# Load order of a gated spectral and MLP token mixer: gate row, tables and an x block moved, and one wait told to the planner

## The chip, the cores and the metric

The kernel runs on one core of a Trainium2 chip. The metric is the device time of one execution in microseconds (us), the median of several runs. Engines are named as the profile does: PE is TensorE (matmuls; PEld its weight loads), DVE is VectorE, ACT is ScalarE, POOL is GpSimd, SP is SyncE, which here only issues DMAs.

## The reference

The input x is 2048 tokens by 512 features. The output is g * a + (1 - g) * b, token by token, where

```
g = sigmoid((x * gate_w).sum(-1))                     # one gate per token
a = irfft2(rfft2(x) * (w_r + 1j * w_i))               # spectral filter over tokens and features
h = layernorm(x);  u = gelu(h^T w1 + b1);  b = (u w2 + b2)^T   # token MLP, 2048 -> 1792 -> 2048
```

All inputs and outputs are bf16. The Fourier transforms are done as radix-4 steps on DVE and matmuls against cosine and sine tables on PE.

## The kernel before, in words

Tokens are split as token = 512 q + 4 a + r, with a on the 128 partitions. A block j = 4 q + r is 128 tokens by 512 features. "Row r" means the four blocks of one r.

**A planner sets the order.** Each step is added as a task with an engine, an estimated duration, reads and writes under symbolic keys, a priority, and buffers that it allocates and frees (`add`, `Plan.order`). The planner runs through time and gives each engine, when it is free, the ready task of the lowest priority number. The result is one fixed list; each engine then runs its instructions in that order. The waits between engines are not the planner's: a layer below places them from the memory ranges that the instructions read and write. So a key that the planner does not know of can still be a wait in the program.

**Loads.** Nearly all loads are tasks of SP (`ld`, `load`, `ld_w1`, `load_wb`, `ld_W`) and go through one DMA queue in the order of their priorities; a few early ones go through ACT's queue. In the first third these are: x by rows; `ta`, the forward tables, one piece per row; w1 in two sets (`wa` holds its first 7 blocks of 128 columns, row by row, and `wb` the next); `flip` and the bias; `tb`, the second forward table; `gw`, the gate row, spread over all partitions; `b2h`; and W, the spectral weights, in many small pieces.

**First third.** Per row r: DVE takes LayerNorm statistics (L487, L488), and normalised blocks h are written by DVE (L521) or ACT (L527). PE accumulates the first MLP product over blocks j (L705), in the order j = 0, 8, 4, 12, 1, 5, 9, 13 and so on. Between these the forward transform runs: DVE combines the four q of a row (L535 to L542), PE multiplies by `ta` (L554 to L557), ACT evicts PSUM (L560), DVE combines again (L566, L567). DVE also multiplies x by the gate row in place (L730, once per row; the only use of `gw`), and ACT sums that to the gate's logit (L735).

**Middle.** A radix-4 over rows on DVE (L585 to L598, then the small L637), a second product on PE with `tb` (L653), eviction on ACT (L660), combination on DVE (L669 to L677), then the spectral multiplication on DVE (L820 to L846). PE fills its time with the MLP: L705, then L1008 with w2.

**First inverse.** A radix-4 on DVE for each half lt (0 and 1 of the spectrum): L590 and L591 write what the even rows r = 0, 2 read, L600 and L601 what the odd rows 1, 3 read. Then PE makes sixteen products `i1(h, r, lt)` (L895, L897 and L898 for even r, L890 for odd r) into two `fa` and two `fb` PSUM buffers, lt 0 in `fa` and lt 1 in `fb`. ACT evicts each (L906 into `ze`, L904 into `zz`); DVE combines the even ones (`zf`, L914 to L920) and makes z (`fq`, L926, L927).

**Last third.** PE makes the last inverse product (`i3`, L967 to L970), ACT scales it by the gate into `B` (L974), DVE combines it (`es`, L989 to L993) and adds it to the MLP's result (`fin2`, L1027), which ACT has evicted (L1014). The last two blocks are finished by DVE (L1021) straight from PSUM. Stores go out on SP, and the last one on ACT's queue.

Of the kernel before, what the change touches and what calls it, by code (L numbers as in the profile page):

```python
# [13 lines left out]
BF16 = mybir.dt.bfloat16  # L14
F32 = mybir.dt.float32

P = 128
S = 2048
D = 512
# [113 lines left out]
class Plan:  # L133
# [11 lines left out]
    def add(self, eng, dur, emit, reads=(), writes=(), prio=0.0, alloc=(), free=(), nbytes=0, after=(), late=0.0):  # L145
        t = Task()
        t.late = late
        t.eng, t.dur, t.emit, t.prio = eng, dur, emit, prio
        t.alloc, t.free, t.nbytes = tuple(alloc), tuple(free), nbytes
        t.users, t.end, t.ready = [], None, 0.0  # L150
        deps = set(after)
        for k in reads:
            if k in self.last_w:
                deps.add(self.last_w[k])
            self.readers.setdefault(k, []).append(t)
        for k in writes:
            if k in self.last_w:
                deps.add(self.last_w[k])
            deps.update(self.readers.get(k, ()))
            self.last_w[k] = t  # L160
            self.readers[k] = []
        deps.discard(t)
        t.deps = deps
        self.tasks.append(t)
        return t
# [73 lines left out]
def tt(n):  # L239
    return 0.07 + n / 1920.0  # L240
# [14 lines left out]
def mm(*ns):  # L255
    return sum(max(n, 120) / 2400.0 + 0.0025 for n in ns)
# [3 lines left out]
def tiny(k):  # L260
    return 0.09 * k + 0.06
# [3 lines left out]
def kernel(  # L265
# [14 lines left out]
    V, A, T = nc.vector, nc.scalar, nc.tensor  # L280
    tabs = {k: nc.inline_tensor(v, name="dft_" + k).ap() for k, v in make_tables().items()}

    rows = "(q a r) d -> a q r d"
    x4 = A_x[0].rearrange(rows, q=4, r=4)
# [17 lines left out]
    add = pl.add  # L302
    t = {}
# [39 lines left out]
    def load(key, shape, dt, src, nbytes, prio=0.0):  # L343
        def emit():
            t[key] = sb(shape, dt, key)
            dma(t[key][:], src)
        return add("SP", 0.5, emit, writes=[key], prio=prio, nbytes=nbytes)

    def ld(keys, dst, src, nbytes, prio, eng="SP"):
        return add(eng, 0.5, lambda: dma(dst(), src, A if eng == "ACT" else None), writes=keys, prio=prio, nbytes=nbytes, after=[a0])  # L350
# [21 lines left out]
    for r in range(4):  # L372
        if r == 0:
            for n, qs in enumerate(XQ):
                ld([("x", 0, q) for q in qs], lambda qs=qs: t["x"][:, qs[0]:qs[-1] + 1:2, 0, :], x4[:, qs[0]:qs[-1] + 1:2, 0, :], 131072 * len(qs), -9 + 0.1 * n)
        else:
            for qs in ((0,), (1,), (2, 3)) if r == 1 else ((0, 1, 2, 3),):
                c = slice(qs[0], qs[-1] + 1)
                ld([("x", r, q) for q in qs], lambda r=r, c=c: t["x"][:, c, r, :], x4[:, c, r, :], 131072 * len(qs), 2 * r - (3 if r == 1 else 0) + 0.01 * qs[0])
        ld([("ta", r)], lambda r=r: t["ta"][:, r, :], tabs["ta"][:, r, :], 163840, 2 * r + (0.6 if r == 1 else 0.2) if r else -0.8)  # L380

    NF = 7
    WB = (0, NF, NF + 4, NFT)
# [23 lines left out]
    def ld_bias():  # L407
        dma(t["b1b"][0:NFT], B_b1.rearrange("(t f) -> t f", f=P))
    add("SP", 0.5, ld_bias, writes=["bias"], prio=7.1, nbytes=4096, after=[a0])
    load("tb", [P, 776], BF16, tabs["tb"], 198656, prio=9)  # L410

    def ld_wb(k, q):
        def emit():
# [10 lines left out]
            add("SP", 0.5, ld_wb(k, q), writes=[("w1", k + 1, 4 * q + r) for r in range(4)], prio=10 + 12 * k + 0.1 * q,  # L424
                nbytes=131072 * (WB[k + 2] - WB[k + 1]), after=after)
    load_wb(0)
    load("gw", [P, D], BF16, gate_w[None, :].to_broadcast([P, D]), 131072, prio=14.5)

    ld(["b2h"], lambda: t["b2h"][:], B_b2.rearrange("(q p r) -> p q r", q=4, r=4), 300000, 14.6)

    wsrc = (A_w_r, A_w_i)

# [39 lines left out]
    for r in range(4):  # L472
# [3 lines left out]
        for b, qs in enumerate(groups):  # L476
# [48 lines left out]
            for j in js:  # L525
                if j in HACT:
                    add("ACT", 0.71, lambda j=j: A.activation(t["h"][:, j // 4, j % 4, :], t["x"][:, j // 4, j % 4, :], ActF.Identity,  # L527
                                                                  bias=t["nmr"][:, j:j + 1], scale=t["rstd"][:, j:j + 1]),
                        reads=xb + [("rstd", *g)] + mvk, writes=[("h", j)], prio=-0.5 + 0.1 * r)
# [19 lines left out]
        for dq in range(4):  # L549
            def fa(r=r, dq=dq):  # L550
# [10 lines left out]
                reads=[("pa", r, dq)], writes=[("X", r, dq)], prio=0, free=["fa"])  # L561
# [69 lines left out]
    for lt in (0, 1):  # L631
# [4 lines left out]
        if lt == 0:  # L636
            add("DVE", 0.15, lambda: V.tensor_copy(t["X"][:, 0, :, :, :, 0], t["fx"][:]), reads=["fx"],  # L637
                writes=[("Z", 0, 0), ("Z", 0, 1)], prio=3.0)
# [6 lines left out]
    for lt in (0, 1):  # L645
        for e in (0, 2, 1, 3):
            for c in range(2):
                tag = ("fa", "fb")[c]
# [7 lines left out]
            for c in range(2):  # L656
                tag = ("fa", "fb")[c]
# [6 lines left out]
            if e >= 2:  # L664
                def tb2(lt=lt, e0=e - 2):
# [14 lines left out]
                    writes=[("B", lt, i) for i in es_], prio=2.5)  # L680
# [47 lines left out]
    for r in range(4):  # L728
# [3 lines left out]
            reads=["gw"], writes=xk, prio=6)  # L732
# [139 lines left out]
    i1t = {}  # L872
    for rs, h in ((0, 0), (0, 1), (1, 0), (1, 1)):
        for r in (rs, rs + 2):
            for lt in range(2):
                tag = ("fa", "fb")[lt]

                def i1(h=h, r=r, lt=lt, tag=tag):
                    if "zz" not in t:
                        t["zz"] = sb([P, 2, 2, 2, 2, 2, 2, P], BF16, "X")  # L880
                        t["ze"] = sb([P, 2, 2, 2, 2, L], BF16, "h")
                    p1 = t["i1", h, r, lt] = ps([P, 2, L], F32, tag, 2)
                    o, w = ti_at(r)
                    ti = t["ti"][:, o:o + w]
                    for v in range(2):
                        d = lambda c: t["B"][:, lt, r, 2 * c + v, h:L:2]
                        if r % 2:
                            for c in range(2):
                                f = (2 * c if lt == 0 else 5 - c) * P
                                T.matmul(p1[:, v], lhsT=d(c), rhs=ti[:, f:f + L], start=(c == 0), stop=(c == 1))  # L890
                        else:
                            n = 129 if r == 0 and lt == 0 else P
                            u = ti[:, 256 * lt:256 * lt + 256]
                            if n > P:
                                T.matmul(p1[:, v], lhsT=d(1), rhs=t["ti"][:, 2816:3072], start=True, stop=False)  # L895
                            else:
                                T.matmul(p1[:, v, n:], lhsT=d(1), rhs=u[:, n:], start=True, stop=True)  # L897
                            T.matmul(p1[:, v, 0:n], lhsT=d(0), rhs=u[:, 0:n], start=(n == P), stop=True)  # L898
                i1t[h, r, lt] = add("PE", mm(*([256] * 4 if r % 2 else [128] * 4)), i1, reads=[("T", lt, r % 2), "ti"], writes=[("i1", h, r, lt)], prio=3, alloc=[tag])

                def i1ev(h=h, r=r, lt=lt):
                    if r % 2:
                        o = t["zz"][:, 1, h, lt, :, :, r // 2, :]
                        A.copy(o, t["i1", h, r, lt][:].rearrange("p v (k a) -> p v k a", k=2))  # L904
                    else:
                        A.copy(t["ze"][:, h, r // 2, lt], t["i1", h, r, lt][:])  # L906
                add("ACT", act(512), i1ev, reads=[("i1", h, r, lt)] + pbk, writes=[("zz" if r % 2 else "ze", h, r, lt)], prio=1.7, free=[tag], after=[lined])

            if r % 2 == 0:
                def zf(h=h, r=r):  # L910
                    e = t["ze"][:, h, r // 2]
                    k0, k1 = (t["zz"][:, 0, h, :, :, k, r // 2, :] for k in range(2))
                    if r == 0:
                        V.tensor_copy(k0[:, :, :, 0], e[:, :, :, 0])  # L914
                        V.tensor_copy(k1[:, :, :, 0], e[:, :, :, P])
                        V.tensor_add(k0[:, :, :, 1:P], e[:, :, :, 1:P], e[:, :, :, P + 1:L])
                        V.tensor_sub(k1[:, :, :, P - 1:0:-1], e[:, :, :, 1:P], e[:, :, :, P + 1:L])
                    else:
                        V.tensor_add(k0, e[:, :, :, 0:P], e[:, :, :, P:L])
                        V.tensor_sub(k1[:, :, :, ::-1], e[:, :, :, 0:P], e[:, :, :, P:L])  # L920
                add("DVE", 2 * tt(512) + (tiny(2) if r == 0 else 0), zf, reads=[("ze", h, r, lt) for lt in range(2)], writes=[("zz", h, r, lt) for lt in range(2)], prio=3.55)

        def fq(rs=rs, h=h):
            z = xph(h)[:, 2048 * rs:2048 * rs + 2048].rearrange("p (q v n) -> p q v n", q=4, v=2)
            a, b = (t["zz"][:, rs, h, i].rearrange("p v k r a -> p k v (r a)") for i in range(2))
            V.tensor_add(z[:, 0:4:3], a, b)  # L926
            V.tensor_sub(z[:, 1:3], a[:, ::-1], b[:, ::-1])  # L927
        add("DVE", 2 * tt(1024), fq, reads=[("zz", h, r, lt) for r in (rs, rs + 2) for lt in range(2)] + [("T", 0, 0), ("T", 0, 1), ("T", 1, 0), ("T", 1, 1)],
            writes=[("z", rs, h)] + ([] if rs else ["pp" if h else "xs"]), prio=3.6)
# [27 lines left out]
    for p in range(NJ // 2):  # L957
# [24 lines left out]
        def es(p=p, j0=j0, late=late, tb2j=tb2j):  # L982
# [8 lines left out]
            V.tensor_sub(s[:, :, 1, :, P - 1:0:-1], e[:, :, :, 1:P], e[:, :, :, P + 1:L])  # L991
            V.tensor_add(o[:, :, 0:4:3], s[:, :, :, 0], s[:, :, :, 1])
            V.tensor_sub(o[:, :, 2:0:-1], s[:, :, :, 0], s[:, :, :, 1])  # L993
        add("DVE", tiny(1) + 4 * tt(512) + (0.3 if late else 0), es, reads=(k1 + ["omg"]) if late else [],
            writes=ko if late else k1, prio=4, alloc=["es"], free=["es"], after=gates if late else ())

        for i, j in enumerate((j0, j1)):
# [78 lines left out]
```

## Time and profile before

| | |
|---|---|
| median of 3 runs | 129.49 us (129.37 to 129.72) |
| the profiled execution | 129.0 us |
| its span, first to last instruction | 127.1 us |
| busy PE, DVE, ACT | 122.3, 114.6, 81.3 us |
| granted PE clock | 1.0 throughout |
| read from HBM, written | 20.86 MB, 2.10 MB |

The durations come from the one profiled execution, whose time lies 0.49 us below the median of the runs and 1.9 us above its own span. In the profile a line number is a line of the kernel; a tile is named without its buffer number. `out<-in` is what an instruction writes and reads. Idle time in brackets stands before the instruction and names what ended it. All DMAs have line L306, that of the helper which issues them.

### The profile page before, as it was taken

The page shows a single profiled execution, that of the slowest core. Times are in us where ns is not written, and L with a number is a line of the kernel's source. Part 1 is how long each engine was busy: PE and PEld are TensorE (multiplying, and loading weights), DVE is VectorE, ACT ScalarE, POOL GpSimd, SP SyncE. Part 2 cuts the span into 40 slices and gives each one's busy share as a digit, 9 for nine tenths or more (in the row PEclk, how much of TensorE's full clock was granted, in tenths as well). Part 3 has the DMA queues.
Part 4 walks back from the last instruction along what each step waited for, and adds up shares of the span by engine and source line. Part 5 has one row for each costly group of instructions (what it writes and reads, how often), then busy time and mean ns, then how long its engine had stood idle before and what let it go on. Part 6 is the DMA issues. An engine that isn't in the chain of part 4 may idle for free.

```text
span 127.1 us, 2153 instructions
## 1 busy us (share of the span) xinstructions
PE 122.3 (96%) x756; PEld 68.9 (54%) x756; DVE 114.6 (90%) x273; ACT 81.3 (64%) x165; POOL 0.2 (0%) x4
## 2 busy tenths in 40 slices
PE   6999999999999999999999999999989999999991
PEld 2345555555555466644445555555667767655590
DVE  2789999996999999999999999999989989999951
ACT  0973789699999999999420004722389999952200
POOL 0000000000000000000000000000000000000000
PEclk9999999999999999999999999999999999999999
DMA  2999999995548946899999900000000000006451
GB/s 69 300 355 291 382 366 368 351 325 106 122 107 256 285 96 143 200 406 415 411 409 406 398 29 0 0 5 0 3 0 0 0 5 0 0 0 248 165 211 44
DMA packets 18219, 23.12 MB, mean 182 GB/s; under 512 B 2190, under 2 KB 15904, under 8 KB 18208
## 3 DMA queue, kind: packets, MB, share of 16 engines
q1 hardware_dynamic: 17616, 22.36, 52.8%
q10 hardware_dynamic: 592, 0.62, 1.6%
q8 instruction: 6, 0.10, 0.3%
q14 instruction: 5, 0.04, 0.1%
HBM read 20.86 MB, written 2.10 MB: 181 GB/s over the span
## 4 chain that ended last, share of the span: by engine, by line
DVE 37%; PE 29%; DMA 21%; SPq 8%; issue 2%; DVEq 0%
PE acc L1008 16%; DMA wa<-in_B_w_dram 12%; SPq L306 8%; DMA gw<-in_gate_w_dram 6%; DVE x L730 4%; DVE xp L828 4%; DVE st L828 3%; DMA x<-in_A_x_dram 3%; DVE st L586 3%; PE acc L705 3%; DVE xp L833 2%; DVE xp L585 2%; DVE B L840 2%; DVE xp L834 2%; PE fb L890 1%
## 5 line engine op out<-in xcount | busy, mean ns | idle before, releaser
L705 PE MATMUL acc<-h,wb 128*128 128x512 bf16 x112 | 26.9, 379 | 0.0
L1008 PE MATMUL acc<-gl,wb 128*128 128x512 bf16 (+1 forms) x98 | 24.6, 371 | 0.0
L1008 PE MATMUL acc<-gl,wa 128*128 128x512 bf16 (+1 forms) x98 | 23.8, 371 | 0.0
L1014 ACT ACTIVATE x<-acc,ombb,omg 128x512 bf16<-128x512 f32 x12 | 9.0, 777 | 21.4 <-PE acc L1008 21.4
L1008 PEld LDWEIGHTS <-wa 128*128 128x128 bf16 x126 | 13.5, 113 | 9.9
L1008 PEld LDWEIGHTS <-wb 128*128 128x128 bf16 x126 | 13.3, 113 | 9.3
L705 PE MATMUL acc<-h,wa 128*128 128x512 bf16 x64 | 17.6, 379 | 0.0
L705 PEld LDWEIGHTS <-wb 128*128 128x128 bf16 x112 | 10.7, 98 | 10.5
L705 PEld LDWEIGHTS <-wa 128*128 128x128 bf16 x112 | 10.3, 98 | 10.4 <-issue 0.8
L487 DVE BATCH_NORM_STATS2 stats<-x 128x6 f32<-128x512 bf16 x14 | 9.5, 678 | 1.9 <-DMA x<-in_A_x_dram 1.9
L560 ACT CAST xp<-fa 128x512 bf16<-128x512 f32 x16 | 9.2, 580 | 2.0 <-PE fa L557 2.0
L735 ACT ACTIVATE x<-x 128x512 bf16<-128x512 bf16 x16 | 10.2, 692 | 0.0
L721 ACT ACTIVATE gl<-acc,b1f 128x512 bf16<-128x512 f32 x11 | 7.9, 719 | 3.5 <-PE acc L705 3.5
L705 PE MATMUL fb<-h,wa 128*128 128x512 bf16 x32 | 9.7, 379 | 0.0
L527 ACT ACTIVATE h<-x,nmr,rstd 128x512 bf16<-128x512 bf16 x11 | 8.4, 807 | 1.1 <-DVE nmr L518 1.1
L705 PE MATMUL fa<-h,wa 128*128 128x512 bf16 x16 | 5.9, 381 | 0.1
L653 PEld LDWEIGHTS <-X 128*128 128x128 bf16 x64 | 4.6, 98 | 2.5 <-DVE X L637 0.7
L974 ACT ACTIVATE B<-fa,g 128x512 bf16<-128x512 f32 x8 | 5.6, 704 | 0.2 <-PE fa L970 0.2
L730 DVE TENSOR_TENSOR x<-x,gw 128x2048 bf16<-128x2048 bf16 x4 | 4.8, 1220 | 1.1 <-DMA gw<-in_gate_w_dram 1.1
L974 ACT ACTIVATE B<-fb,g 128x512 bf16<-128x512 f32 x8 | 5.7, 712 | 0.0
L356 PE MATMUL fa<-xp 128*128 128x512 bf16 x10 | 4.4, 632 | 1.2 <-DVE xp L317 1.2
L660 ACT CAST X<-fb 128x512 bf16<-128x512 f32 x8 | 5.1, 636 | 0.0
(169 smaller groups left out, 232.8 us busy)
## 6 DMA issues: line engine op xcount, KB each, us to landing
wb<-in_B_w_dram SPq DMA_DIRECT2D x11, 512.0 KB
wa<-in_B_w_dram SPq DMA_DIRECT2D x7, 512.0 KB
wa<-in_B_w_dram SPq DMA_DIRECT2D x2, 896.0 KB
wb<-in_B_w_dram SPq DMA_DIRECT2D x4, 384.0 KB
out_dram<-x SPq DMA_DIRECT2D x3, 512.0 KB
x<-in_A_x_dram SPq DMA_DIRECT2D x2, 512.0 KB
wa<-in_B_w_dram SPq DMA_DIRECT2D x2, 448.0 KB
rot<-dft_ti SPq DMA_DIRECT2D x1, 768.0 KB
```

The source lines that it names most:

```text
L306: (eng or nc.sync).dma_start(out=out_ap, in_=in_ap)
L487: V.bn_stats(out=t["stats"][:, j, :], in_=t["x"][:, j // 4, j % 4, :])
L527: add("ACT", 0.71, lambda j=j: A.activation(t["h"][:, j // 4, j % 4, :], t["x"][:, j // 4, j % 4, :], ActF.Identity, bias=t["nmr"][:, j:j ...
L560: add("ACT", act(512), lambda r=r, dq=dq: A.copy(xe(r)[:, :, :, dq, :], t["pa", r, dq][:]), reads=[("pa", r, dq)], writes=[("X", r, dq)], ...
L705: T.matmul(t["u", ft][:], lhsT=w[:, j // 4, j % 4, c * P:(c + 1) * P], rhs=t["h"][:, j // 4, j % 4, :], start=(j == jorder[0]), stop=(j == ...
L721: gelus.append(add("ACT", act(512, 1) , lambda ft=ft: A.activation(t["gl"][:, ft, :], t["u", ft][:], ActF.Gelu_apprx_tanh, bias=t["b1f"][: ...
L730: add("DVE", tt(2048), lambda r=r: V.tensor_mul(t["x"][:, :, r, :], t["x"][:, :, r, :], t["gw"][:, None, :].to_broadcast([P, 4, D])), read ...
L735: A.activation(t["x"][:, q, r, :], t["x"][:, q, r, :], ActF.Copy, accum_out=t["glog"][:, 4 * q + r:4 * q + r + 1])
L828: V.tensor_mul(o, xs, w)
L974: A.activation(eo_v(p)[:, n], t["i3", j][:], ActF.Copy, scale=t["g"][:, j:j + 1])
L1008: T.matmul(t["y", j, m][:, cs], lhsT=w[:, o, 512 * q + r:512 * q + 512:4], rhs=t["gl"][:, ft, cs], start=(ft == 0), stop=(ft == NFT - 1))
L1014: A.activation(tbuf(j).rearrange("p h d -> p (h d)"), t["y", j, 0][:], ActF.Identity, bias=t["ombb2"][:, j:j + 1], scale=t["omg"][:, j:j + 1])
```

## The change

Four edits. The third x row is loaded ahead of the second part of w1's row 1 (and the planner's numbers for the x and `ta` loads are written out in tuples). The `ta` pieces of rows 2 and 3 move behind the loads of x row 3 and of w1's row 3. `gw` moves from behind the first `wb` set to before it, and `tb` from before that set to behind it. The inverse product of r = 2 is said to read ("T", lt, 1) too, the key of the odd rows. And the planned duration of `es` is 0.2 longer; that number is only the planner's.

```diff
-                ld([("x", r, q) for q in qs], ..., 2 * r - (3 if r == 1 else 0) + 0.01 * qs[0])
-        ld([("ta", r)], ..., 2 * r + (0.6 if r == 1 else 0.2) if r else -0.8)
+                ld([("x", r, q) for q in qs], ..., (0, -0.9 if len(qs) > 1 else -1 + 0.01 * qs[0], 2.503, 4.6)[r])
+        ld([("ta", r)], ..., (-0.8, 2.505, 6.3, 7.3)[r])
...
-    load("tb", [P, 776], BF16, tabs["tb"], 198656, prio=9)
+    load("tb", [P, 776], BF16, tabs["tb"], 198656, prio=14.7)
...
-    load("gw", [P, D], BF16, gate_w[None, :].to_broadcast([P, D]), 131072, prio=14.5)
-    ld(["b2h"], ..., 300000, 14.6)
+    load("gw", [P, D], BF16, gate_w[None, :].to_broadcast([P, D]), 131072, prio=7.2)
+    ld(["b2h"], ..., 300000, 14.9)
...
-  i1t[h, r, lt] = add("PE", ..., i1, reads=[("T", lt, r % 2), "ti"], ...)
+  i1t[h, r, lt] = add("PE", ..., i1, reads=[("T", lt, r % 2), "ti"] + ([("T", lt, 1)] if r == 2 else []), ...)
...
-        add("DVE", tiny(1) + 4 * tt(512) + (0.3 if late else 0), es, ...)
+        add("DVE", 0.2 + tiny(1) + 4 * tt(512) + (0.3 if late else 0), es, ...)
```

The queue's order of loads from the first `ta` on, before and after (w1 a, b: its row 1 for q = 0, 1 and q = 2, 3; w1 2, 3: its rows 2 and 3):

```
before: ta0  w1a  w1b  ta1  x2   ta2  w1_2  x3  ta3  w1_3  flip  bias  tb   wb x4       gw  b2h
after:  ta0  w1a  x2   ta1  w1b  w1_2  x3   ta2  w1_3  flip  bias  gw   ta3  wb x4       tb  b2h
```

On PE the instructions are the same in kind and order; the product `i1(1, 0, 1)` changes places with `i1(0, 2, 1)`. ACT's evictions follow that. On DVE the combinations `zf` of r = 2 come after those of r = 0 of both halves, and in the last third two `es` are followed by two `fin2`.

More of the change, by code (lines that the diff above doesn't have):

```diff
@@ L378 @@
                 c = slice(qs[0], qs[-1] + 1)
-                ld([("x", r, q) for q in qs], lambda r=r, c=c: t["x"][:, c, r, :], x4[:, c, r, :], 131072 * len(qs), 2 * r - (3 if r == 1 else 0) + 0.01 * qs[0])
-        ld([("ta", r)], lambda r=r: t["ta"][:, r, :], tabs["ta"][:, r, :], 163840, 2 * r + (0.6 if r == 1 else 0.2) if r else -0.8)
+                ld([("x", r, q) for q in qs], lambda r=r, c=c: t["x"][:, c, r, :], x4[:, c, r, :], 131072 * len(qs), (0, -0.9 if len(qs) > 1 else -1 + 0.01 * qs[0], 2.503, 4.6)[r])
+        ld([("ta", r)], lambda r=r: t["ta"][:, r, :], tabs["ta"][:, r, :], 163840, (-0.8, 2.505, 6.3, 7.3)[r])
     NF = 7
@@ L426 @@
     load_wb(0)
-    load("gw", [P, D], BF16, gate_w[None, :].to_broadcast([P, D]), 131072, prio=14.5)
-    ld(["b2h"], lambda: t["b2h"][:], B_b2.rearrange("(q p r) -> p q r", q=4, r=4), 300000, 14.6)
+    load("gw", [P, D], BF16, gate_w[None, :].to_broadcast([P, D]), 131072, prio=7.2)
+    ld(["b2h"], lambda: t["b2h"][:], B_b2.rearrange("(q p r) -> p q r", q=4, r=4), 300000, 14.9)
     wsrc = (A_w_r, A_w_i)
@@ L898, in i1 @@
                             T.matmul(p1[:, v, 0:n], lhsT=d(0), rhs=u[:, 0:n], start=(n == P), stop=True)
-                i1t[h, r, lt] = add("PE", mm(*([256] * 4 if r % 2 else [128] * 4)), i1, reads=[("T", lt, r % 2), "ti"], writes=[("i1", h, r, lt)], prio=3, alloc=[tag])
+                i1t[h, r, lt] = add("PE", mm(*([256] * 4 if r % 2 else [128] * 4)), i1, reads=[("T", lt, r % 2), "ti"] + ([("T", lt, 1)] if r == 2 else []), writes=[("i1", h, r, lt)], prio=3, alloc=[tag])
                 def i1ev(h=h, r=r, lt=lt):
@@ L993, in es @@
             V.tensor_sub(o[:, :, 2:0:-1], s[:, :, :, 0], s[:, :, :, 1])
-        add("DVE", tiny(1) + 4 * tt(512) + (0.3 if late else 0), es, reads=(k1 + ["omg"]) if late else [],
+        add("DVE", 0.2 + tiny(1) + 4 * tt(512) + (0.3 if late else 0), es, reads=(k1 + ["omg"]) if late else [],
             writes=ko if late else k1, prio=4, alloc=["es"], free=["es"], after=gates if late else ())
```

## The prediction

> **What bounds the kernel now.** I read the page's busy times first, then the timeline of TensorE (PE), then the list of waits, and last the timelines of VectorE (DVE) and ScalarE (ACT) around the waits found.
>
> ```profile
> PE 122.3 (96%) x756; PEld 68.9 (54%) x756; DVE 114.6 (90%) x273; ACT 81.3 (64%) x165; POOL 0.2 (0%) x4
> ```
>
> PE is at work in 96% of the span, and the change touches neither a matmul nor its shape. So the time can change only where PE stands still, and it stands still little. I took PE's starts one after the other: a 128x512 matmul starts 0.216 us after the one before it, a 128x128 one 0.055 us. What exceeds that is lost. From the first real matmul (5.56 us) to the last (124.06) the losses add up to 3.5 us, and half of that lies in six places: 0.23 at 6.9, 0.19 at 12.0, 0.14 at 16.7, 0.27 at 32.4, 0.33 at 44.8 and 0.55 at 93.1. The last three, in PE's timeline (start, length, what, idle and its releaser):
>
> ```profile
> 32.38 0.22 PE L556 MATMUL fa<-rot,gl 128*128 128x128 bf16 x1
> 32.69 0.23 PE L557 MATMUL fa<-rot,gl 128*128 128x128 bf16 x1
> ...
> 43.25 1.67 PE L705 MATMUL acc<-h,wb 128*128 128x512 bf16 x7
> 45.09 0.40 PE L653 MATMUL fa<-tb,X 128*128 128x128 bf16 x4 [0.16 <-DVE X L637]
> ...
> 93.00 0.22 PE L898 MATMUL fb<-rot,B 128*128 128x128 bf16 x1
> 93.61 0.23 PE L897 MATMUL fb<-rot,B 128*128 128x128 bf16 x1 [0.39 <-DVE B L601]
> ```
>
> Read the starts, not the bracket (the bracket counts from the modelled end). 32.69 - 32.38 - 0.055 = 0.26. Seven matmuls from 43.25 would end their turn at 44.76; L653 starts at 45.09: 0.33. 93.61 - 93.00 - 0.055 = 0.55. Sum 1.14 us. DVE releases all three. Why it is late is seen in its own timeline:
>
> ```profile
> 28.96 0.69 DVE L536 TENSOR_TENSOR gl<-x 128x1024 bf16<-128x1024 bf16 x1
> 30.74 1.23 DVE L730 TENSOR_TENSOR x<-x,gw 128x2048 bf16<-128x2048 bf16 x1 [1.09 <-DMA gw<-in_gate_w_dram]
> ...
> 32.22 0.42 DVE L542 TENSOR_TENSOR gl<-st 128x512 bf16<-128x512 bf16 x1
> ...
> 44.78 0.25 DVE L637 CAST X<-fx 128x32 bf16<-128x32 f32 x1
> ...
> 92.87 0.69 DVE L601 TENSOR_TENSOR B<-st 128x1024 bf16<-128x1024 bf16 x1
> ```
>
> DVE idles 1.09 us for the gate row (L730), and from there to L637 it has no other gap. L542 (end 32.64) releases L557, L637 (end 45.03) releases L653. So the first two stalls hang on one late 128-KB load.
>
> **The loads.** In the trace's landing records the loads of one queue end in the order of their issue, the slowest of the 16 rings at: w1 row 1 first part 12.63, second part 13.80, `ta` 1 14.25, x row 2 15.75, `ta` 2 16.19, w1 row 2 18.64, x row 3 20.11, `ta` 3 20.56, w1 row 3 23.05, flip 23.25, `tb` 23.70, first wb 25.12, last wb 30.02, gw 30.72. The steps between them are each load's price in the stream. In the new order: x row 2 at 12.63 + 1.50 = 14.1, `ta` 1 14.6, w1's second part + 1.17 = 15.75, w1 row 2 18.2, x row 3 19.7, `ta` 2 20.1, w1 row 3 22.6, flip 22.8, gw + 0.7 = 23.5, `ta` 3 23.9, the wb's 0.3 later than before, `tb` about 30.8. The bytes and the number of DMAs are the same, and every issue still waits on the load eight before it, so the W loads behind them shift by at most 0.3.
>
> Who needs them: gw at 29.6 (6 us early now); `ta` 1 at 16.41 (1.8 early, was 2.2); w1's second part at 16.88, where PE starts block j=9 (1.1 early, was 3.1); `ta` 2 at 24.8; `ta` 3 at 32.16; `tb` at 45.09, L653 (14 early); the first wb at 35.9. SP has nothing else in line there. x rows 2 and 3 come earlier to a DVE that is busy anyway (first use 16.24 and 21.87): worth nothing. So the moves cost nothing, and only w1's second part gives up real cover; if that goes, each microsecond of delay is one of PE.
>
> **The gate row.** DVE starts L730 at 29.65 instead of 30.74. Two later DVE steps wait for ACT's eviction of row 2 (ended 32.75, DVE then at 33.7) and row 3 (36.16, DVE at 36.2, and ACT too is 0.25 earlier): covered. So L542 ends at 31.55, ahead of L557's turn at 32.43: +0.26. L637 ends at 43.94, PE wants L653 at 44.76 - 0.26 = 44.50: +0.33. PE is 0.59 early from there. Does it keep that? The next bound is ACT. It gains 0.25 behind PE's first gain, then 0.27 where it idles for PE:
>
> ```profile
> 49.03 0.69 ACT L721 ACTIVATE gl<-acc,b1f 128x512 bf16<-128x512 f32 x1 [0.27 <-PE acc L705]
> ...
> 51.98 0.65 ACT L660 CAST X<-fb 128x512 bf16<-128x512 f32 x1
> ```
>
> 0.52 in all. PE's L653 at 50.35 to 52.77 wait for buffers that ACT evicts, with 0.12 to 0.18 of room, and PE runs only 0.07 further ahead than ACT: it just fits. DVE's L669 at 52.66 started 0.03 after ACT's eviction (51.98 + 0.65), so from there DVE keeps 0.52 of its 1.09. From 53 to 91 PE waits for nothing that is short: w2 blocks land 1.85 us or more ahead of first use, and L741 has 0.98 on ACT.
>
> **The first inverse.** Before, PE takes product (h0, r2, lt1) right after (h0, r0, lt1); its wait is on L601, the last step of the radix-4, though r2's rows were written earlier: L600 and L601 write strided rows whose span covers them. The new read of ("T", lt, 1) tells the planner this. In the built program PE's rows are the same in kind, but (h1, r0, lt1) has changed places with (h0, r2, lt1): the wait on L601 now stands behind two products and one L1008 and four L890 matmuls, 1.1 us later. In the new time PE comes there at 93.58, and L601 ends at 93.55 - 0.52 = 93.0. So the 0.55 goes. What is late next: ACT evicts each product (0.48 us from one to the next) into `ze` and `zz`, and PE waits for the buffer two before. From 91.24 on ACT needs sixteen evictions and one L1014 (0.68): 8.3 us, ended at 99.5; PE's buffer waits keep 0.04 to 0.2 of room by the same sum. Behind the moved wait stand PE's own next products and, through them, ACT's evictions; it is met before PE reaches it, so nobody waits. DVE now combines r0 of both halves first and then waits for the eviction of (h0, r2, lt1), at 95.6: it idles 0.5 there, and `z` of half 1 is ready at 99.6 instead of 99.85. PE's first L967 needs the first half of it at 99.67 (100.81 - 1.14) and the second at 99.84: 0.2 of room. I take no loss, with 0.2 as the upper bound.
>
> **The planner's 0.2 for `es`.** No instruction changes; DVE's tail order does: two `es`, then two L1027 sums. Same work, 18.2 us from 102.59 to 120.83; starting 0.6 earlier it ends at 120.2, ahead of need except 0.15 at the first L1021, which has 0.8 behind it. The sums come up to 1.3 us later, and with them one 512-KB store (115.5 instead of 114.51), which nothing waits for: the last 512-KB store landed at 124.04, the last of all at 126.19. Cost 0.
>
> **Sum.** 0.26 + 0.33 + 0.55 = 1.14 us. The profiled execution took 129.0 (span 127.1 and 1.9 around it): it becomes 127.9. The median of the runs is 0.49 above the profiled one; I keep that: 129.49 - 1.14 = 128.35, rounded 128.4.
>
> **Rivals.**
> (a) One of the gains is taken back by ACT. For it: ACT's room is 0.04 to 0.2 us at a dozen buffer waits. Against: in all of them ACT itself moves with PE. If the swap gives nothing (or another wait on `B` stands in its place), PE's 0.59 shrinks to DVE's 0.52: 129.0. If the buffers hold PE to ACT's old pace only in part, 0.3 to 0.6 are lost: 128.7 to 129.0. The Trainium skill's page "Perfetto Trace Analysis" (section "Optimization Strategy") says that consistent bubbles can mean that SBUF or PSUM is too small for the next tile; by it this case would be the likelier. The trace speaks against it for before: none of the three stalls was released by ACT.
> (b) Nothing moves: the stalls are taken up by some wait that the profile shows as covered, total gain under 0.39: 129.1 to 129.9. Against: PE has no second row of waits within 0.5 us.
> (c) Slower: w1's second part comes late. It decides from a landing after 16.8; from 18.4 on it eats both gains and is seen as slower. For it: the first part of the same row took 2.8 us of the stream where the second took 1.17. Price: rings spread 2.1 us between the first and the last; if the three loads did not overlap their ends, it would land at 15.75 + 2 x 2.1 = 19.95, PE would stand for 3.1 us, and the time be 131.5. Against: 448 KB landed 1.17 us behind its predecessor, with the ends overlapped. The Trainium skill's page "DMA: Bandwidth & Descriptors" (section "Anatomy of one DMA") fits one DMA of the GpSimd path as 2.0 us plus its bytes over 436 GB/s; paid three times in a row, as an estimate, that would be 8.6 us and slower still, and the trace's 1.17 contradicts such a sum for queued loads.
>
> **How the numbers follow.** Forecast 0.60, (a) 0.20, (b) 0.08, (c) 0.12. A difference of 0.3% (0.39 us) is about what a measurement of this kernel can tell from no change, so the forecast and (a) count as faster: 0.80. The forecast's own range is 128.1 to 128.6 (0.2 lost; 0.25 gained, should unprofiled runs have waited more for gw). With (a) it reaches 129.1, and a margin of 0.1 for the runs' scatter gives 128.0 to 129.2.
>
> **What would show it.** In the new profile: L730 with no wait for gw, at 29.6; L557 0.06 behind L556; no idle at L653; the wait on L601 gone from PE's list; L1014 and i3 (L967) starting 1.1 earlier. Wrong would be: idle of PE at about 16.9 with a wait for `wa`; new gaps of PE at L890 or L897 released by ACT; the first L967 waiting for DVE.

## The result and the profile after

The changed kernel takes 127.75 us (median of 5 runs, 127.68 to 128.01) against 129.37 for the kernel before on the same chip. The ratio is 0.9899, 95% interval 0.9867 to 0.9931, so the gain is 1.31 us (0.89 to 1.72). A second series on another occasion gave 127.95 against 129.11 and 0.9898 (0.9864 to 0.9932). Forecast were 1.14 us and 128.4.

The profiled execution took 128.01 us with a span of 126.2. Its busy times, its chain that ended last (shares by engine), and PE's whole list of waits:

```profile
PE 121.4 (96%) x743; PEld 68.9 (55%) x756; DVE 114.4 (91%) x273; ACT 81.0 (64%) x165; POOL 0.2 (0%) x4
```

```profile
PE 93%; DMA 3%; ACTq 1%; issue 1%; DVE 0%
```

```profile
PE fa L356 <- DVE xp L317: 1.2, 1, 1.2
```

Before, the same chain read "DVE 37%; PE 29%; DMA 21%": it ran over the gate row and the stalls. Now it is PE's own work. The shares alone prove little: e3 below has no stall either, and its chain reads "PE 56%; DMA 30%; SPq 11%". PE's one listed wait is that of its warm-up matmuls for a memset. Thirteen matmul records are missing from this trace (743 of 756), and each looks like a gap of 0.05 us in PE's timeline, or like 0.22 too much between two starts; those are not stalls.

The three places of the prediction, in PE's timeline (start, length, what):

```profile
32.14 0.22 PE L556 MATMUL fa<-rot,gl 128*128 128x128 bf16 x1
32.20 0.22 PE L557 MATMUL fa<-rot,gl 128*128 128x128 bf16 x1
...
43.94 1.03 PE L705 MATMUL acc<-h,wb 128*128 128x512 bf16 x4
44.80 0.39 PE L653 MATMUL fa<-tb,X 128*128 128x128 bf16 x4
...
93.42 0.60 PE L890 MATMUL fa<-rot,B 128*128 128x256 bf16 x4
93.86 0.22 PE L897 MATMUL fb<-rot,B 128*128 128x128 bf16 x1
```

L557 follows L556 by 0.06. Four L705 from 43.94 end their turn at 44.80, and L653 starts there. The moved product starts at 93.86, four L890 (0.11 each) behind 93.42. And DVE around them:

```profile
29.27 0.69 DVE L536 TENSOR_TENSOR gl<-x 128x1024 bf16<-128x1024 bf16 x1
29.87 1.22 DVE L730 TENSOR_TENSOR x<-x,gw 128x2048 bf16<-128x2048 bf16 x1
...
31.34 0.42 DVE L542 TENSOR_TENSOR gl<-st 128x512 bf16<-128x512 bf16 x1
...
43.91 0.26 DVE L637 CAST X<-fx 128x32 bf16<-128x32 f32 x1
...
92.57 0.69 DVE L601 TENSOR_TENSOR B<-st 128x1024 bf16<-128x1024 bf16 x1
...
95.97 0.42 DVE L919 TENSOR_TENSOR X<-h 128x512 bf16<-128x512 bf16 x1 [0.41 <-ACT h L906]
```

L730 no longer waits (the gate row landed at 22.26). L601 ends at 93.26, 0.60 ahead of the product that reads it.

**Two executions must be set at the same start.** Row 1's first L554 on PE started at 16.41 us before and at 16.72 after, for reasons that lie ahead of the change: row 0's first L554 differs as much (11.23 and 11.54), and no load that was moved had landed by then. From there to PE's last start it is 107.65 us before (124.06 - 16.41) and 106.48 after (123.20 - 16.72): 1.17 gained, where 1.14 was forecast. This stretch turned out to be the sharpest instrument of the study: in all seven profiles in which PE has no stall in it, it is 106.48 or 106.49. (0.14 us that PE stands ahead of j=9 in every profile, before and after, are part of it; a stall there is counted over them.)

| kernel | first L554 of row 1 | from it to PE's last start | over 106.48 | PE's stalls in it, added |
|---|---|---|---|---|
| before | 16.41 | 107.65 | 1.17 | 0.26 + 0.33 + 0.55 = 1.14 |
| after | 16.72 | 106.48 | 0 | none |
| e1 | 16.64 | 107.81 | 1.33 | 0.74 + 0.56 = 1.30 |
| e2 | 16.52 | 107.02 | 0.54 | 0.19 + 0.33 = 0.52 |
| e3 | 16.78 | 106.48 | 0 | none |
| e4 | 16.83 | 107.85 | 1.37 | 0.17 + 0.28 + 0.33 + 0.56 = 1.34 |
| e5 | 16.66 | 106.48 | 0 | none |
| e6 | 16.66 | 110.50 | 4.02 | 2.42, and 1.59 of slow matmuls |
| e7 | 16.86 | 106.49 | 0.01 | none |
| e8 | 16.97 | 106.49 | 0.01 | none |
| e9 | 16.81 | 106.49 | 0.01 | none |
| e10 (after again) | 16.89 | 106.48 | 0 | none |
| e11 | 16.98 | 107.34 | 0.86 | 0.84 |
| e12 | 17.15 | 107.13 | 0.65 | 0.63 |

### The profile page after: what moved, and what is told of

Same layout as the page of the kernel before. It is cut to its first block, busy times and chain, and to the rows that moved or that the text cites. A ratio compares the mean times of both kernels' runs of the same rounds, so it can differ in the third digit from the quotient of the medians.

```text
span 126.2 us, 2141 instructions
## 1 busy us (share of the span) xinstructions
PE 121.4 (96%) x743; PEld 68.9 (55%) x756; DVE 114.4 (91%) x273; ACT 81.0 (64%) x165; POOL 0.2 (0%) x4
## 4 chain that ended last, share of the span: by engine, by line
PE 93%; DMA 3%; ACTq 1%; issue 1%; DVE 0%
PE acc L1008 32%; PE acc L705 30%; PE fb L705 5%; PE fb L1008 5%; PE fa L705 3%; DMA wa<-in_B_w_dram 3%; PE fa L554 2%; PE fb L653 2%; PE fa L653 2%; PE fa L890 2%; PE fb L890 1%; PE fa L555 1%; ACTq L306 1%; PE fa L557 1%; PE fa L556 1%
## 5 line engine op out<-in xcount | busy, mean ns | idle before, releaser
L705 PE MATMUL acc<-h,wb 128*128 128x512 bf16 x108 | 25.9, 379 | 0.1
L1008 PE MATMUL acc<-gl,wb 128*128 128x512 bf16 (+1 forms) x94 | 24.0, 371 | 0.2
L1008 PE MATMUL acc<-gl,wa 128*128 128x512 bf16 (+1 forms) x97 | 23.8, 371 | 0.1
L1008 PEld LDWEIGHTS <-wa 128*128 128x128 bf16 x126 | 13.5, 113 | 9.9
L1008 PEld LDWEIGHTS <-wb 128*128 128x128 bf16 x126 | 13.3, 113 | 9.3
L705 PE MATMUL acc<-h,wa 128*128 128x512 bf16 x62 | 17.5, 382 | 0.1
L705 PEld LDWEIGHTS <-wb 128*128 128x128 bf16 x112 | 10.7, 98 | 10.5
L705 PEld LDWEIGHTS <-wa 128*128 128x128 bf16 x112 | 10.3, 98 | 10.7 <-DMA wa<-in_B_w_dram 1.0
L705 PE MATMUL fb<-h,wa 128*128 128x512 bf16 x31 | 9.5, 379 | 0.1
L705 PE MATMUL fa<-h,wa 128*128 128x512 bf16 x16 | 6.1, 393 | 0.1
L653 PEld LDWEIGHTS <-X 128*128 128x128 bf16 x64 | 4.7, 98 | 2.1
L511 ACT ACTIVATE rstd<-mv,eps 128x1 f32<-128x1 f32 (+1 forms) x11 | 3.2, 293 | 2.9 <-DVE mv L488 2.4
```

Source lines behind the costliest of these rows:

```text
L653: T.matmul(pb[:, k % 2, k // 2], lhsT=t["X"][:, lt, EX[e], c, k, :], rhs=tbl(k, c), start=True, stop=True)
L705: T.matmul(t["u", ft][:], lhsT=w[:, j // 4, j % 4, c * P:(c + 1) * P], rhs=t["h"][:, j // 4, j % 4, :], start=(j == jorder[0]), stop=(j == ...
L1008: T.matmul(t["y", j, m][:, cs], lhsT=w[:, o, 512 * q + r:512 * q + 512:4], rhs=t["gl"][:, ft, cs], start=(ft == 0), stop=(ft == NFT - 1))
```

## The experiments

### e1 to e4: the change in its parts

Four kernels made from the one before: the gate row alone (e1), the planner's new read alone (e2), both (e3), and all the other moved loads (e4). They share 28 runs of the kernel before (median 129.3).

```diff
 e1, e3: -    load("gw", ..., 131072, prio=14.5)
         +    load("gw", ..., 131072, prio=7.2)
 e2, e3: -  reads=[("T", lt, r % 2), "ti"]
         +  reads=[("T", lt, r % 2), "ti"] + ([("T", lt, 1)] if r == 2 else [])
 e4:     the new numbers of x, ta, tb and b2h, and nothing else
```

> The kernel before with the gate row's load moved ahead of the first wb set, nothing else; the order on PE, DVE and ACT stays as before. Theory S (the time is PE's starts plus its stalls, and each stall goes with its wait): the two stalls at L557 and L653 go and PE is 0.59 us early at L653, but at the first inverse DVE is only 0.52 early, so the wait on L601 grows to 0.62: net gain 0.52 us against the kernel before. Theory L (the order of loads as a whole, x and tables too, is what helps, by a quieter start): under 0.3. Theory B (ACT's evictions take the gain back at L653): under 0.3, with new PE idle behind L660.

> The kernel before with the one added read of the r = 2 product alone, loads as before. Theory S: the stalls at L557 and L653 stay (0.26 and 0.33), the wait on L601 goes; gain 0.55 us. Theory B: ACT's evictions or the later sums for z hold PE, new idle at L890 or L967, gain under 0.3.

> The kernel before with both: gate row early and the added read; x, ta and tb loads as before, es as before. Theory S: 1.14 us, the same as the whole change. Theory L: 0.3 to 0.5 less than the whole change, so a gain of about 0.8 to 1.1 where the whole change has 1.3 to 1.6.

> The kernel before with the x, ta, tb and b2h loads reordered as in the whole change, the gate row left late, the added read left out. Theory S: all three stalls as before, gain 0.0 within 0.1. Theory L: gain of 0.3 to 0.5 us. If w1's second part came too late: slower, with PE idle at 16.9.

| | median us (runs) | ratio, 95% interval | gain us |
|---|---|---|---|
| e1 gate row | 128.59 (12) | 0.9944, 0.9924 to 0.9964 | 0.72 (0.47 to 0.98) |
| e2 inverse | 128.70 (11) | 0.9949, 0.9923 to 0.9975 | 0.66 (0.32 to 1.00) |
| e3 both | 128.01 (6) | 0.9887, 0.9858 to 0.9917 | 1.46 (1.07 to 1.84) |
| e4 other loads | 129.07 (12) | 0.9988, 0.9957 to 1.0018 | 0.16 (-0.23 to 0.56) |

The gain is in two edits and it adds up: 0.72 + 0.66 = 1.38 against 1.46 for both and 1.31 for the whole change. Theory S stands. Theory L falls with e3: without the other moves it gains as much as the whole change, and its stretch is the same 106.48. (e4's interval alone would still leave room for L's 0.3 to 0.5.) B falls, since ACT took nothing back in e3.

The traces say the same stall by stall. In e2's timeline of PE the inverse's stall is gone and the first two are there:

```profile
32.49 0.22 PE L556 MATMUL fa<-rot,gl 128*128 128x128 bf16 x1
32.74 0.23 PE L557 MATMUL fa<-rot,gl 128*128 128x128 bf16 x1
...
45.13 0.40 PE L653 MATMUL fa<-tb,X 128*128 128x128 bf16 x4 [0.17 <-DVE X L637]
```

In e1 (PE's timeline again) it is the other way round, but there is a stall that the profile of before did not have and the theories did not expect:

```profile
23.71 0.38 PE L705 MATMUL fb<-h,wa 128*128 128x512 bf16 x1
24.67 0.18 PE L685 MATMUL fa<-flip,b1b 128*128 128x14 bf16 x1 [0.58 <-DMA b1b<-in_B_b_dram]
...
93.39 0.22 PE L898 MATMUL fb<-rot,B 128*128 128x128 bf16 x1
94.00 0.23 PE L897 MATMUL fb<-rot,B 128*128 128x128 bf16 x1 [0.39 <-DVE B L601]
```

L685 stood 24.67 - 23.71 - 0.216 = 0.74 for the bias, a load that e1 does not move: everything queued ahead of it is as before. In the profile before, the bias landed at 23.46 and PE took L685 at 23.69 without a wait; in e1 it landed at 24.63. In e3, whose loads have e1's order, it landed at 23.32. So this load came later from one execution to the next by more than its room. In the changed kernel, which moves two `ta` pieces behind it, the bias landed at 22.03 and PE took L685 at 24.00, 1.97 us of room (1.46 in e10). That is a use of the other moves which neither e4's median nor my prediction shows.

### e5: the gate row alone put back

```diff
 after   -    load("gw", ..., prio=7.2)
         +    load("gw", ..., prio=14.5)
```

> The changed kernel with one load put back: the gate row again behind the four wb loads. The instructions of PE, DVE and ACT keep the order of the changed kernel. Theory S (the gain is the three stalls and nothing else): the wait of L730 for the gate row is back, 1.0 to 1.5 us, and with it PE's stalls at L557 (0.2 to 0.3) and L653 (0.33); the stall at L897 stays gone. 127.75 + 0.6 = 128.35, or 0.7 below before. Theory L (the order of the loads is worth something as a whole, whichever of them moves): 127.75 to 127.9, since all other loads stay where the change put them.

Measured: 128.57 (12 runs, 127.73 to 130.40) against 129.32; ratio 0.9935 (0.9906 to 0.9965), a gain of 0.84 us (0.45 to 1.22). That is 0.5 less than the whole change, as S says, though the intervals overlap. But the profiled execution (127.95) has no stall at all. The gate row landed in time there. DVE's L730 in e5, and in e4 for contrast:

```profile
30.06 1.23 DVE L730 TENSOR_TENSOR x<-x,gw 128x2048 bf16<-128x2048 bf16 x1 [0.17 <-DMA gw<-in_gate_w_dram]
```

```profile
31.35 1.23 DVE L730 TENSOR_TENSOR x<-x,gw 128x2048 bf16<-128x2048 bf16 x1 [1.27 <-DMA gw<-in_gate_w_dram]
```

With the load at the end of the `wb` set, L730 started at 30.06, 30.74, 30.78 and 31.35 in four profiles (e5, before, e2, e4), and the stalls at L556, L557 and L653 together cost 0, 0.59, 0.52 and 0.78. So the worth of moving the gate row is not one number. It is paid in some executions and not in others, and 0.59 was one draw of it. In e5 the row was used with a room of 0.17: L542 ended at 31.96 and PE took L557 at 32.13.

### e6, e11, e12: w1's second part late, the price of rival (c)

Three kernels made from the changed one. They issue that load later: behind w1's row 2 (e12), between the halves of x row 3 (e11, which makes two loads of that row), behind x row 3 (e6).

```diff
 e6, at x row 3   -  dma(t["x"][:, :, 3, :], ...)
                  +  dma(t["x"][:, :, 3, :], ...); dma(t["wa"][:, 2:4, 1, :], ...)
 e11              +  dma(x, q 0 and 1); dma(wa); dma(x, q 2 and 3)
 e12              +  dma(wa); dma(x)
```

> The changed kernel with the second part of w1's row 1 issued behind w1's row 2 and x row 3, the price that rival (c) of the prediction put on a late landing. In the changed kernel's trace it landed at 14.88, w1 row 2 at 17.28 and x row 3 at 18.79, and PE starts j=9 at 17.19. So here it lands at 18.8. Theory S (PE has no slack in front of it or behind): PE stands at the first L705 of j=9 for 1.6 us with a wait for wa, and the time is 127.75 + 1.6 = 129.35. Theory C (a microsecond of PE at 17 us is partly taken up later, because DVE and ACT run ahead meanwhile and shorten later waits): loss under 1.0, time under 128.8.

> As e6, but w1's second part is issued between the two halves of x row 3 (which becomes two loads). It should land at 18.0 to 18.8, and PE stand 0.9 to 1.6 us at j=9. In e6 PE stood 2.4 us there, and the nine matmuls behind it started 0.427 apart instead of 0.216, at a granted clock of 0.5: 1.5 us more. Theory G (an idle time of over some length takes the clock down, and it was passed in e6 and not in e8, whose 0.88 left the clock at 1.0): if the length is under 1.4, time 127.75 + 1.3 + 1.5 = 130.5; if it is above, 127.75 + 1.3 = 129.1, with matmuls at 0.216 right behind the stall. Rival H (the slow matmuls of e6 were a chance of that profile): 129.1 and e6's median must then be explained otherwise.

> As e6, but w1's second part is issued right behind w1's row 2 and ahead of x row 3: one place later than in the changed kernel. It should land at 17.3 to 18.0, and PE wants it at 17.1 to 17.2. Theory S: a stall of 0.1 to 0.9 at j=9, each us of it one of the time, the clock stays at 1.0: 127.85 to 128.6. Theory C (taken up later): 127.75.

| | median us (runs) | ratio, 95% interval | load landed (slowest ring) | PE's stall at j=9 |
|---|---|---|---|---|
| e12 | 128.58 (10) | 0.9955, 0.9927 to 0.9983 | 18.21 | 0.63 |
| e11 | 129.36 (10) | 1.0009, 0.9981 to 1.0036 | 18.25 | 0.84 |
| e6 | 132.12 (6) | 1.0176, 1.0112 to 1.0239 | 19.50 | 2.42 |

e11 and e12 go by S: the stretch grew by 0.86 and 0.65, the stall and no more, and nothing took it up later; theory C falls. By the medians, against 127.95 for the changed kernel beside them (e10), e12 lost 0.63 and e11 1.41. The profiled execution of e11 was one of its faster ones (129.06), and how long PE stood in the others is not known. e6 went further than either theory: 4 us lost for a load 2.4 us late. PE's timeline there (start, length, what):

```profile
16.94 0.22 PE L557 MATMUL fa<-rot,gl 128*128 128x128 bf16 x1
19.55 0.61 PE L705 MATMUL fa<-h,wa 128*128 128x512 bf16 x1 [2.39 <-DMA wa<-in_B_w_dram]
19.95 1.91 PE L705 MATMUL acc<-h,wa 128*128 128x512 bf16 x4
21.66 0.63 PE L705 MATMUL fb<-h,wa 128*128 128x512 bf16 x1
...
22.73 0.42 PE L705 MATMUL fb<-h,wa 128*128 128x512 bf16 x1
```

and the same stretch by windows (window, its length, PE busy, granted PE clock, DMA share, GB/s):

```profile
17.00:19.50 2.50, 0.16 (x3) 0.98 1.07 375
19.50:20.50 1.00, 0.95 (x3) 0.50 1.05 376
20.50:21.50 1.00, 1.00 (x4) 0.50 1.09 350
21.50:22.50 1.00, 1.00 (x4) 0.50 1.10 353
22.50:23.50 1.00, 1.00 (x8) 0.85 1.09 351
```

PE is at work in each window from 19.5 on, but it does half as much: the 128x512 matmuls start 0.427 us apart ((21.66 - 19.95) / 4) instead of 0.216, and the granted clock reads 0.50. From the first L705 at 19.55 to the one at 22.98 it took 3.43 us; the changed kernel takes 1.84 for the same instructions (1.59 less). 2.42 + 1.59 = 4.01, and the stretch grew by 4.02. The trace's clock records read 1.00 from 5.72, 0.50 from 19.38 to 22.79, and 1.00 again: the clock went down during PE's idle time, and it came back about 3 us after PE's restart. e11's 0.84 did not do it: its matmuls behind the stall start 0.216 apart. e11 was meant to stall for 1.3, so if the length decides, it lies between 0.84 and 2.42, no closer.

The length may not be all. The half clock lasted 3.41 us, and the 13.66 us from 5.72 to 19.38 are four times that. In each of the 13 traces that hold clock records, the time from the first record to the next change is a whole number of such steps (36 x 3.41 before, 35 x 3.41 after), while the first record begins anywhere from 4.17 to 7.13. So the clock seems to change only at steps of 3.41 us, which lie differently in each execution, and the same stall could cost the clock in one execution and not in another. No run tests that. Five of e6's six runs lie above 131.6, which speaks against rival H, a chance of one profile. The sixth, at 130.38, lies where the idle time alone would put it (127.95 + 2.42 = 130.4), but it was not profiled.

The Trainium skill's page "TensorE: Matmul & The Clock Gate" (section "What's actually happening") has the clock at half after at least one idle window of some 3.4 us. The half clock itself and a length of 3.41 us agree with this trace, a wholly idle window does not: of the 3.41 us ahead of the drop PE was idle for 2.22 (17.16 to 19.38).

### e7: without the planner's 0.2 for es

```diff
 after   -        add("DVE", 0.2 + tiny(1) + 4 * tt(512) + (0.3 if late else 0), es, ...)
         +        add("DVE", tiny(1) + 4 * tt(512) + (0.3 if late else 0), es, ...)
```

> The changed kernel without the planner's 0.2 for es. Only DVE's order in the last third differs: one L1027 sum stands ahead of the second es again. The prediction put this edit at nothing: 127.75, within 0.2. Rival: the order of the tail matters, by the 0.15 at the first L1021 up to the 0.8 behind it: 127.9 to 128.5.

Measured: 128.16 (9 runs) against 129.32; ratio 0.9907 (0.9875 to 0.9938), not to be told from 0.9899. The median alone would lie in the rival's range. But the stretch is 106.49, and from PE's last start to the end of the span it is 3.0 us in both kernels, so the profile shows no loss in the tail. The edit costs and brings nothing that these runs can tell, as forecast.

### e8, e9: two attempts at a faster version

From row 1 on PE waits for nothing that the profile lists, so without less work on PE only an earlier start could bring more. A w1 load of row 0 (q = 2) goes from ACT's queue to SP's, behind the two x loads (e8) or between them (e9). ACT then loads its table 0.48 us earlier.

```diff
 e8   -    w1_0(0, 2, ALL, "ACT", -8.8)
      +    w1_0(0, 2, ALL, "SP", -8.85)
 e9   +    w1_0(0, 2, ALL, "SP", -8.95)
```

> An attempt at a faster version: the changed kernel, with one load of w1's row 0 (q = 2, 224 KB) taken from ACT's queue and put on SP's behind the two x loads of row 0. In the changed kernel's trace ACT issues it from 2.60 to 3.05 and then loads its table (3.08, 1.28 us), DVE waits 0.55 for ACT's L511 at 4.58 and 0.58 for an x load at 6.08. Theory S (from 12 us on PE has no idle time worth naming, so a start that is earlier is an end that is earlier): L511 starts at 4.40 instead of 4.58, and the x load of q = 1 has one load less beside it, so PE's first L705 and its row 0 come 0.2 to 0.4 earlier: 127.35 to 127.55. Rival: the load of w1 lands too late for j=8 (it landed at 6.67 and is needed at 7.3 to 7.7; 0.75 later in issue brings 7.4), or PE's first L705 hangs on w1's first block, which landed at 5.70 and does not move: 127.75 to 128.1.

> The second attempt at a faster version. As in e8 the w1 load of row 0, q = 2, goes from ACT's queue to SP's, but one place further ahead, between the two x loads. In e8 PE's first L705 started at 5.34 (5.74 in the changed kernel), and all of it was lost at j=8, where PE stood 0.88 for that load (landed 7.85, issued at 3.35). Here it is issued at 2.89 and the x load of q = 3 at 3.35. Theory S (an earlier start is an earlier end): w1 lands at 6.9 to 7.3, PE wants it at 6.95, and 0.1 to 0.4 of the earlier start is kept: 127.35 to 127.65, against 127.75 for the changed kernel. Rival: the load's rings spread so wide (6.08 to 7.85 in e8) that one place ahead is not enough, PE stands 0.3 to 0.9 at j=8: 127.8 to 128.5.

> The changed kernel itself, beside e9, e11 and e12, so that they are compared on one chip. All theories: 127.7 to 128.1. Theory J (the run-to-run spread of the kernel before is the landing time of the gate row, which reaches PE there and does not here): its runs lie within 0.5 us, those of the kernel before within 1.5.

Measured: e8 128.55 (ratio 0.9954, 0.9932 to 0.9976), e9 128.31 (0.9938, 0.9910 to 0.9966), and the changed kernel beside e9 127.95 (0.9898). Neither is faster, and e8 lies above even its rival's range. In e8 PE's first L705 did start at 5.34, and the stall that the rival names took it all (PE's timeline of e8):

```profile
5.34 0.38 PE L705 MATMUL fa<-h,wa 128*128 128x512 bf16 x1
5.56 1.02 PE L705 MATMUL acc<-h,wa 128*128 128x512 bf16 x4
6.42 0.59 PE L705 MATMUL fb<-h,wa 128*128 128x512 bf16 x2
7.90 0.39 PE L705 MATMUL fa<-h,wa 128*128 128x512 bf16 x1 [0.88 <-DMA wa<-in_B_w_dram]
```

In e9 that load landed in time (6.46) and nothing was won either. There, as in the changed kernel's second profile, the first three or four matmuls were slow. PE's timeline of that second profile, e10:

```profile
5.55 0.59 PE L705 MATMUL fa<-h,wa 128*128 128x512 bf16 x1
5.93 1.63 PE L705 MATMUL acc<-h,wa 128*128 128x512 bf16 x4
7.40 0.59 PE L705 MATMUL fb<-h,wa 128*128 128x512 bf16 x2
7.83 0.38 PE L705 MATMUL fa<-h,wa 128*128 128x512 bf16 x1
```

Its first seven matmuls take 5.55 to 7.83, 2.28 us, where 7 x 0.216 = 1.51 are enough in e8. The slow ones start up to 0.43 apart, as in e6 at a half clock. The windows view gives 1.00 for them, but it gives 1.00 wherever the trace has no clock record, and e10's first record begins at 7.13, just where the spacing falls (7.18). In the changed kernel's first profile both are at 6.57, in the profile before the record begins at 5.70, so "granted PE clock 1.0 throughout", said of the kernel before, holds from there on. So two things set the start, and both differ from run to run: when the clock comes up, and when the x load of q = 1 lands (5.5 to 6.6). An edit of 0.2 us does not show in that.

Theory J of e10 is not shown. The changed kernel's six runs do lie within 0.47 us, and those of the kernel before within 1.62 (28 runs, the slowest left out). But e5 with its late gate row and e9 with its early one scatter alike, within 1.24 (11 runs, the slowest left out) and 1.18 (12 runs).

## Why the prediction was right, and where not

**The three stalls: right.** All three are gone, and the stretch gained 1.17 where the sum said 1.14. e1 to e3 show that each edit removes its own. Two sizes on the way there were off and changed nothing. The losses of PE before add up to about 2.0 us and not 3.5 (redone from the starts, with 0.216, 0.109 and 0.055 for 512, 256 and 128 columns), so the six places named are most of them and not half. And DVE came to the end of L601 0.60 us earlier, counted from row 1's first L554 (93.55 - 16.41 before, 93.26 - 16.72 after), where the prediction left it 0.52; so e1's stall at L897 stayed at 0.56 and did not grow to 0.62.

**ACT's thin room: right.** Rival (a) fell: PE waits for no eviction. The least room of PE on one, worked out from starts and ends as the prediction did, is 0.05 us between 45 and 52 us and 0.05 between 92 and 98. It holds because PE and ACT move together.

**The new wait of DVE and `z`: right.** L919 stood 0.41 at 95.97 for ACT's eviction; 0.5 was forecast, and 95.6 with 0.31 of start on top. L967 starts at 99.95, straight behind its L1008. Of the 0.2 taken as the upper bound nothing was lost.

**`es`: right**, by e7.

**w1's second part: not late, as said, but its price was wrong.** It landed at 14.88 (forecast 15.75) and PE took j=9 at 17.19. The step "each microsecond of delay is one of PE" holds to 0.84 us (e11). At 2.42 each microsecond cost 1.66, since the clock went down as well (e6). For the prediction's 3.1 us the loss would then have been above 3.1, and 131.5 too low.

**"The median of the runs is 0.49 above the profiled one; I keep that": the step that failed.** The forecast lay 0.60 and 0.40 above the 127.75 and 127.95 measured (128.35 before rounding). A part of it was the base: 129.49 was the median of three runs, and the later series of the kernel before, of 5 to 29 runs, gave 129.37, 129.30, 129.32 and 129.11. In the series with 129.11 that is nearly all: its medians differ by 1.16 (129.11 - 127.95), where 1.14 was forecast. In the first, of five runs each, they differ by 1.62 (1.31 by the ratio of the runs). What is left of the 0.49, 0.11 to 0.37, would fit that one profiled execution: its start, 16.41, is the earliest of fourteen profiles (16.41 to 17.15, the middle 16.8), so 0.39 ahead of the middle. That is argued and not shown, since no other execution of the kernel before was profiled. The profile after already had a usual start, so its time (128.01) should have been compared with the median directly: it lies 0.26 above it. The gate row's varying lateness adds to the gain in some executions beyond 0.59 (e4: 0.78) and takes from it in others (e5: 0). How much of the gap between 1.17 and the 1.31 of the runs that is, these runs do not tell; the interval holds both.

## What to carry to other kernels

Where one engine is at work in 96% of the span, list its starts, add up what exceeds the usual spacing, and see who releases each place: here three stalls of a quarter to half a microsecond, from one late load and one product placed too early, were the whole gain, and they added up. Set two profiles at a common event behind the start-up before comparing them; that gave stalls to 0.03 us where the times of the runs scatter by 0.5 to 2. And give a load that PE waits for more room than one profile shows, for its landing moves by a microsecond from run to run, and a stall that is long enough can also cost the clock.

## What was not expected of the hardware

With an idle time of 2.4 us PE's granted clock went to 0.50 for 3.41 us (1.59 us of work lost), while 0.84 us left it alone. In 13 traces the clock changed only at whole steps of 3.41 us from its first record, whose place moved between 4.17 and 7.13. A load is there when its slowest ring is: in e12 the first of the 16 landed at 16.71 and the last at 18.21, and PE started at 18.25; in e8 6.08 and 7.85, and PE at 7.90. And one and the same load at the same place in the queue, the gate row, let L730 start at 30.06 in one execution and at 31.35 in another, after a wait in both.
